# Batch 1's attention moved from the head into chunk 0's first layer

## Chip, cores, metric

The kernel runs on one core of a Trainium2 chip. The metric is device time in microseconds of one launch; lower is better. A core has TensorE (PE), VectorE (DVE), ScalarE (ACT), GpSimd (POOL) and SyncE (SP), which here only issues DMAs, and 16 DMA engines that all queues share.

## What is computed

Eight batches, eight heads, 576 positions, head size 64, float32. Linear attention without a softmax, a root-mean-square norm per head, then a gated feed-forward layer whose weights arrive as float64:

```python
kv = np.einsum('bhsd,bhse->bhde', k, v)
out = np.einsum('bhsd,bhde->bhse', q, kv)
rms = np.sqrt(np.mean(out * out, axis=-1, keepdims=True) + 1e-06)
x = (out / rms * g_norm)            # then (B,H,S,D) -> (B*S, H*D): 4608 tokens of 512
gate = 1.0 / (1.0 + np.exp(-(x @ w_gate)))      # w_gate, w_val: 512 x 1536
result = (gate * (x @ w_val)) @ w_out           # w_out: 1536 x 512
```

## The kernel before

**Chunks.** The 4608 tokens are nine chunks of 512. Chunk 0 needs batch 0, chunk 1 the end of batch 0 and most of batch 1, and so on. `xT_ring` holds three chunks of normed attention, features on the partitions. A chunk has a first layer (gate and value, 12 blocks of 128 hidden features) and a second layer. Chunk 0 is computed plainly: a block is 8 matmuls of 128x128 by 128x512 (`Plain.mm`, L561), the second layer 48 more (L808). Chunks 1 to 8 use a scheme with fewer, smaller products (L932 and L1036) of sums: sums of weights (`w1_sums` at L741, `w_form` at L1007), sums of x (`x_sums` at L830) and sums of hidden values (`h_sums` at L722). Most of these sums are GpSimd's.

**Two forms of attention.** In the *early form* (`attention`, L276 to L342) a pair of heads goes through k-v matmuls (KV), a copy (KVO), TensorE transposes of q (Q), a copy (QO), the product with q (U), Square (SQ), a sum (SUM), Sqrt (ROOT), the norm by VectorE (NORM), TensorE transposes (X) and copies into xT (XO). Batches 0 and 1 (`NE = 2 * NHP`, eight pairs) are done so in the head. In the *late form* (`feed`) a batch's k-v matmuls come at once (L366, L372), ScalarE copies them (`kv_copies`, 12 copies), VectorE transposes q in 32x32 blocks (`turn`, L383), and two pairs at a time go through `two_pairs`: `u_mm` (L407), `u_square`, two `u_sum`, `u_root`, two `u_norm` by VectorE (L425), two `x_turn` (VectorE transposes, then DMAs into xT). Batches 2 to 7 are done so beside the fast first layers of chunks 1 to 6. The result of L366 and of `u_mm` lies in one region of PSUM, `at`, with one buffer.

**Conversion of weights.** A unit is 1 MB of float64: 12 units hold the gate and value weights of one block f of chunk 0 each, then 6 hold two blocks of w_out each. SP loads a unit into one of three `st` buffers; five VectorE steps (L179, L190, L200, L204, L211 or L213) and two of ScalarE (L184, L195) make float32 of it. The last step of a unit lets SP issue the load three units on. Chunk 0's block f needs unit f converted.

**Order.** The engines run their instructions in the order in which the program writes them. The head is written out by hand as a string of tokens: `KV0` is a step of pair 0, `c1.3` and `a1.0` are conversion steps of unit 1, `w2` loads unit 2, `b0.1.2` is a matmul of block 0, `CG`, `CV`, `S` and `M` put the gate and value of blocks 0 and 1 aside and finish them later, `warm10` stands for ten matmuls of the identity with itself, which keep TensorE busy. Blocks 0 to 3 of chunk 0 are in it. Then come blocks 4 to 11 by `plain`, with a conversion step after six of the eight matmuls of each; the gate (ACT) and the product (DVE) of a block follow in the next block (`late`). After block 8 stand batch 2's k-v matmuls, after block 10 the call `w1_sums(0)`, after block 11 `w1_sums(1)`; these write their sums over `h_more`, where batch 2's k and v had been loaded. `w1_sums(2)` follows in the second layer, when all conversions have been written.

**Buffers.** Early k, v, q tiles are in the pool `first`; when its last reader is issued, `h_main` (hidden values, three tiles) and `h_more` take its place.

Of the kernel before, what the change touches and what calls it, by code (L numbers as in the profile page):

```python
# [20 lines left out]
def kernel(  # L21
# [57 lines left out]
    first = first_ctx.__enter__()  # L79


    NE = 2 * NHP
    pairs = {n: {} for n in range(B * NHP)}

    def load_kv(n):
        if n >= NE:
            return
        b, h0 = n // NHP, 2 * (n % NHP)
        for name, src in (("k", k), ("v", v)):
            t = first.tile([NP, 2, NJ * HD], FP32, tag=name, name=name)  # L90
            nc.sync.dma_start(out=t, in_=src[b, h0:h0 + 2].rearrange("h (p j) d -> p h (j d)", j=NJ))
            pairs[n][name] = t

    def load_q(n):
        if n >= B * NHP:
            return
        b, h0 = n // NHP, 2 * (n % NHP)
        if n < NE:
            t = first.tile([NP, NJ, 2, HD], FP32, tag="q", name="q")
            for e in range(2):  # L100
                nc.sync.dma_start(out=t[:, :, e, :], in_=q[b, h0 + e].rearrange("(p j) d -> p j d", j=NJ))
        else:
            t = sb.tile([NP, 2, NJ * HD], FP32, tag="q", name="q", bufs=1)
# [5 lines left out]
    def load_late(b):  # L109


        if b >= B:
            return
        mains = {}
        for n in range(NHP):
            for name, src in (("k", k), ("v", v)):
                mains[n, name] = t = kv_place(len(mains))
                nc.sync.dma_start(out=t.rearrange("p (h c) -> p h c", h=2),
                                  in_=src[b, 2 * n:2 * n + 2, 0:S4].rearrange("h (p j) d -> p h (j d)", j=NK4))
        rest = kv_place(len(mains))  # L120
        for i, src in enumerate((k, v)):
            for r in range(2):
                nc.scalar.dma_start(out=rest[PH * r:PH * r + PH, GH * i:GH * i + GH].rearrange("p (h d) -> p h d", d=HD),
                                  in_=src[b, NHP * r:NHP * r + NHP, S4:S].rearrange("h p d -> p h d"))
        kv_late[b] = mains, rest

# [91 lines left out]

    conversion = [convert(u) for u in range(len(units))]

    to_convert = deque((u, i) for u in range(5, len(units)) for i in range(5))

    def convert_step():

# [40 lines left out]
    def attention(n, at_ps):  # L265
# [12 lines left out]

        def kv_out():
            nc.vector.tensor_copy(out=kv, in_=d["kv"][:, 0, 0:HD])  # L280
            load_kv(n + 4)

        def q_mm():
            d["q"] = ps = at_ps("q")
# [5 lines left out]
        def q_out():  # L290
            d["qT"] = qTs[:, n % 2, 0:S]
            nc.scalar.copy(out=d["qT"].rearrange("p (i n) -> p i n", i=2), in_=d["q"][:, :, 0:JH * NP])
            for i in (n + 4,) if n + 4 < NE else (NE,) if n == NE - 1 else ():
                load_q(i)

        def u_mm():

# [56 lines left out]
    def feed(b):  # L354
# [25 lines left out]
        def turn(n, e):  # L380

            w_ = NJ * HD
            nc.vector.transpose(qTs[0:NP, n % 2, w_ * e:w_ * e + w_],  # L383
                                pairs[n]["q"][:, e].rearrange("p (j i c) -> p i j c", i=NC, c=QB))
            if e == 1:
                load_q(n + 1)

        def two_pairs(n0):

# [38 lines left out]
            def x_turn(i):  # L428
# [6 lines left out]
                for j in range(2):  # L435
# [7 lines left out]
                                                          in_=xTs[p0:p0 + QB, i, :, s0:s0 + n_])  # L443
                            s0 += n_

            return ([u_mm, u_square, lambda: u_sum(0), lambda: u_sum(1), u_root, lambda: u_norm(0), lambda: u_norm(1)] +
                    [lambda i=i: x_turn(i) for i in range(NC)])

        def turns_of(n):
# [3 lines left out]
        kv = [kv_mm] + [lambda i=i: kv_copies(i, range(3)) for i in range(2 * NC)]  # L453
        t0, t1, t2, t3 = (turns_of(n0 + i) for i in range(4))
        u0, u1 = two_pairs(n0), two_pairs(n0 + 2)
        steps_ = t0 + t1 + t2 + t3 + u0 + u1[:7]
        first = [(p, steps_[i]) for p, i in (((0, 0), (5, 1), (9, 2), (21, 3), (25, 8), (26, 9), (28, 4), (28, 5), (30, 10), (30, 11), (32, 6), (42, 12), (48, 13), (49, 7), (50, 14), (52, 15), (53, 16), (53, 17), (56, 18), (57, 19), (57, 20), (60, 21), (60, 22), (62, 23)) if b == 2 else
                                             ((5, 0), (8, 1), (22, 2), (24, 3), (28, 8), (29, 4), (29, 5), (30, 9), (33, 10), (33, 11), (35, 6), (36, 12), (41, 13), (47, 7), (47, 14), (51, 15), (51, 16), (54, 17), (56, 18), (56, 19), (56, 20), (61, 21), (64, 22), (64, 23)) if b == 3 else
# [64 lines left out]
    def mm_ps():  # L523
        return bank((2, 3, 0, 1)[next(turns) % 4])
# [45 lines left out]

    late = deque()

    def plain(c, u, ps):
# [17 lines left out]

    order = """
        warm10 KV0 Q0 KVO0 QO0 w1 warm3 U0 SQ0 KV1 SUM0 ROOT0 Q1 KVO1 NORM0 QO1 warm3 U1 SQ1 SUM1 X0 c0.0 c0.1
        XO0 ROOT1 NORM1 warm13 KV2 warm2 Q2 KVO2 a0.0 c0.2 X1 a0.1 c0.3 c0.4 QO2 w2 warm6 U2 SQ2 KV3 Q3 b0.0.0 b0.1.0
        KVO3 XO1 QO3 w3 U3 SUM2 KV4 Q4 ROOT2 NORM2 SQ3 SUM3 ROOT3 X2 XO2 b0.0.1 b0.1.1 b0.0.2 NORM3 X3 KVO4 QO4
        U4 c1.0 a1.0 c1.1 a1.1 c1.2 c1.3 b0.1.2 KV5 Q5 KVO5 XO3 b0.0.3 b0.1.3 SQ4 c1.4 w4 SUM4 QO5 U5 CG0 CV0
        KV6 Q6 b1.0.0 ROOT4 NORM4 X4 b1.1.0 b1.0.1 b1.1.1 SQ5 SUM5 ROOT5 KVO6 QO6 XO4 U6 NORM5 X5 c2.0 c2.1 a2.0
        c2.2 b1.0.2 KV7 Q7 SQ6 SUM6 a2.1 b1.1.2 ROOT6 c2.3 b1.0.3 XO5 b1.1.3 KVO7 QO7 U7 c2.4 NORM6 CG1 X6 CV1  # L600
        b2.0.0 SQ7 XO6 b2.1.0 b2.0.1 c3.0 SUM7 ROOT7 b2.1.1 c3.1 a3.0 a3.1 NORM7 X7 XO7 c3.2 c3.3 c3.4 b2.0.2
        b2.1.2 b2.0.3 c4.0 S0 S1 b2.1.3 M0 G2 M1 b3.0.0 b3.1.0 a4.0 E2 c4.1 a4.1 c4.2 c4.3 b3.0.1 b3.1.1 b3.0.2
        b3.1.2 b3.0.3 b3.1.3 c4.4
    """
    blks, copies = {}, {}
    warm = mm0_ps()
    for token in order.split():
        name = token.rstrip("0123456789.")
        n = [int(i) for i in token[len(name):].split(".")]
        f = n[0]  # L610
        if name == "b":
            if f not in blks:
                if f == 3:
                    psum_ctx.__exit__(None, None, None)
                    psum = ctx.enter_context(tc.tile_pool(name="psum", bufs=1, space=bass.MemoryType.PSUM))
                    ps = (mm_ps(), mm_ps())
                else:
                    ps = (mm0_ps() if f else warm, mm0_ps())
                blks[f] = Plain(0, F_ORDER[f], ps)
            blks[f].mm(n[1], n[2])  # L620
        elif name == "CG":
            copies[f, 0] = sg_tile()
            nc.scalar.copy(out=copies[f, 0], in_=blks[f].ps[0])
        elif name == "CV":
            copies[f, 1] = sg_tile()
            nc.vector.tensor_copy(out=copies[f, 1], in_=blks[f].ps[1])
        elif name == "S":
            nc.scalar.activation(out=copies[f, 0], in_=copies[f, 0], func=AF.Sigmoid)
        elif name == "M":
            nc.vector.tensor_tensor(out=gv_tile(0, F_ORDER[f]), in0=copies[f, 1], in1=copies[f, 0], op=ALU.mult)  # L630
        elif name == "G":
            blks[f].gate()
        elif name == "E":
            blks[f].end()
        elif name in ("c", "a"):
            conversion[f][name][n[1]]()
        elif name == "w":
# [145 lines left out]
    w1_more[0] = [more[:, i] for i in range(10)]  # L783
    w1_more[1] = [more[:, i] for i in range(10, 18)] + [sgs[-1][:, GH * i:GH * i + GH] for i in range(2)]
    spare_sg = sgs.pop()
    second_batch = feed(2)
    load_late(2)
    late.extend([blks[3].gate, blks[3].end])
    for f in range(4, NFT):
        if f == NFT - 1:  # L790
            last = at_ps()
            plain(0, f, (last[:, 0], last[:, 1]))
        else:
            plain(0, f, (mm_ps(), mm_ps()))
        if f == 8:
            second_batch[0][0]()
        elif f == 9:
            for step in second_batch[0][1:]:
                step()
        elif f == 10:  # L800
            w1_sums(0)
        elif f == NFT - 1:
            w1_sums(1)

    ps = [mm_ps() for _ in range(G // P)]
# [359 lines left out]
```

## Time and profile before

| | us |
|---|---|
| median of three runs | 1016.38 (1016.28 to 1017.71) |
| the profiled execution's own time | 1015.84 |
| its span | 1014.1 |
| TensorE busy | 1006.5 (99%) |
| VectorE busy | 727.1 (72%) |
| GpSimd busy | 598.9 (59%) |
| ScalarE busy | 350.2 (35%) |
| last early attention step on TensorE (L333) | 52.7 |
| batch 2's k-v matmuls (L366, L372) | 98.0 to 100.4 |
| chunk 0's second layer on TensorE (L808) | 121.1 to 162.3 |
| chunk 1 | 162.3 to 269.9 |

The span runs from the first to the last instruction of one profiled execution. A timeline row reads: start, duration, engine, line, operation, output<-input, shape; in brackets the idle time of the engine before it and what ended that. One matmul of the program is two in the trace[...]. An entry "PE" is the multiplication, "PEld" the loading of weights beside it. The pitch of one instruction to the next can be less than its duration where two overlap, so sums are made from starts.

### The profile page before, as it was taken

The numbers are of one execution on the slowest core, as the hardware profiler recorded it, in microseconds if no ns is written. First come the engines' busy times: TensorE is split into PE (matmuls) and PEld (weight loads), VectorE is DVE, ScalarE is ACT, GpSimd is POOL, SyncE is SP. The second block draws the span as 40 slices with busy tenths as digits, with TensorE's granted clock in tenths as the row PEclk, the third lists the DMA queues.
The fourth block names the chain that finished last, engine by engine and source line by source line (L and its number), as shares of the span: only waits on it lengthen the run. The fifth ranks groups of instructions, "written<-read, shape, count | busy, mean of one in ns | idle before, by whom it ended". The sixth has DMA issues, their size and how long they took to land.

```text
span 1014.1 us, 18347 instructions
## 1 busy us (share of the span) xinstructions
PE 1006.5 (99%) x6914; PEld 828.0 (82%) x6914; DVE 727.1 (72%) x1211; ACT 350.2 (35%) x609; POOL 598.9 (59%) x965
## 2 busy tenths in 40 slices
PE   9999999999999999999999999999999999999998
PEld 8644447888888888888888888888888888888887
DVE  4899899899668846775678666866688556755672
ACT  4654422442154304441254115421453033213320
POOL 0001999998448642967177706962496439744963
PEclk9999999999999999999999999999999999999999
DMA  9975314644778468646765577556764546444514
GB/s 264 278 237 191 125 42 157 220 143 163 235 245 301 165 194 262 225 159 200 232 234 194 150 229 248 195 160 190 235 214 153 178 155 208 161 156 158 211 59 124
DMA packets 101128, 193.89 MB, mean 191 GB/s; under 512 B 27408, under 2 KB 74128, under 8 KB 101040
## 3 DMA queue, kind: packets, MB, share of 16 engines
q0 software_dynamic: 20976, 112.87, 32.9%
q1 hardware_dynamic: 72896, 77.75, 25.2%
q10 hardware_dynamic: 7168, 2.10, 0.9%
q8 instruction: 55, 0.90, 0.4%
q14 instruction: 33, 0.27, 0.1%
HBM read 160.04 MB, written 25.56 MB: 183 GB/s over the span
## 4 chain that ended last, share of the span: by engine, by line
PE 74%; POOL 2%; issue 0%; DVE 0%; POOLq 0%
PE mm L932 47%; PE mm L1036 24%; PE at L407 2%; PE at L366 1%; POOL h L722 1%; POOL w_ring L1007 0%; POOL h_more L722 0%; PE at L372 0%; POOL w L770 0%; DVE sg L902 0%; POOL w L1007 0%; POOLq L1007 0%
## 5 line engine op out<-in xcount | busy, mean ns | idle before, releaser
L932 PE MATMUL mm<-xs,w 128*128 128x256 f32 x1428 | 332.0, 380 | 0.0
L932 PEld LDWEIGHTS mm<-xs,w 128*128 128x128 f32 x1428 | 270.4, 190 | 37.4 <-DVE temps L902 0.3
L932 PE MATMUL mm<-xT,w 128*128 128x256 f32 x948 | 230.0, 380 | 0.0
L932 PEld LDWEIGHTS mm<-xT,w 128*128 128x128 f32 x948 | 179.4, 190 | 25.5 <-issue 1.0
L902 DVE TENSOR_TENSOR sg<-sg,mm 128x512 f32<-128x512 f32 (+1 forms) x176 | 100.8, 599 | 93.1 <-PE mm L932 45.7
L770 POOL DMA_DIRECT2D w<-kept x84 | 46.9, 558 | 190.7 <-PE mm L932 188.4
L1036 PE MATMUL mm<-w,h 128*128 128x256 f32 x630 | 143.4, 379 | 0.9 <-POOL h L894 0.5
L1036 PEld LDWEIGHTS mm<-w,h 128*128 128x128 f32 x630 | 119.5, 190 | 17.9 <-POOL h L894 0.9
L898 ACT COPY temps<-mm 128x512 f32<-128x512 f32 (+1 forms) x128 | 66.0, 537 | 190.0 <-PE mm L932 94.9
L894 POOL TENSOR_TENSOR h<-h,sg 128x512 f32<-128x512 f32 x72 | 97.6, 1372 | 50.3 <-DVE h L902 33.2
L722 POOL TENSOR_TENSOR h<-h 128x128 f32<-128x128 f32 x216 | 113.4, 537 | 16.5 <-DVE h_more L722 13.1
L1036 PE MATMUL mm<-w,h_more 128*128 128x256 f32 x474 | 108.2, 379 | 0.0
L891 ACT ACTIVATE sg<-sg 128x512 f32<-128x512 f32 x96 | 59.7, 630 | 131.4 <-DVE sg L902 131.4
L1036 PEld LDWEIGHTS mm<-w,h_more 128*128 128x128 f32 x474 | 90.1, 190 | 12.2
L898 ACT COPY sg<-mm 128x512 f32<-128x512 f32 (+1 forms) x112 | 57.1, 510 | 91.2 <-PE mm L1036 48.8
L722 POOL TENSOR_TENSOR h_more<-h 128x128 f32<-128x128 f32 x120 | 58.5, 490 | 33.9 <-DVE h L894 29.6
L561 PE MATMUL mm<-xT,w 128*128 128x512 f32 x176 | 77.7, 594 | 0.0
L902 DVE TENSOR_TENSOR temps<-temps,mm 128x512 f32<-128x512 f32 (+1 forms) x96 | 59.2, 617 | 25.5 <-PE mm L1036 17.2
L902 DVE TENSOR_TENSOR temps<-mm,temps 128x512 f32<-128x512 f32 (+1 forms) x64 | 39.8, 621 | 50.6 <-PE mm L1036 23.6
L898 ACT COPY h<-mm 128x512 f32<-128x512 f32 x48 | 28.1, 585 | 125.5 <-PE mm L932 110.5
L902 DVE TENSOR_TENSOR sg<-mm,sg 128x512 f32<-128x512 f32 (+1 forms) x64 | 39.6, 618 | 43.7 <-PE mm L932 21.9
L741 POOL TENSOR_TENSOR h_more<-w 128x256 f32<-128x256 f32 x10 | 12.8, 1299 | 97.4 <-PE at L366 97.4
(132 smaller groups left out, 1324.5 us busy)
## 6 DMA issues: line engine op xcount, KB each, us to landing
w<-kept POOLq DMA_DIRECT2D x42, 896.0 KB, 5.0
w<-kept POOLq DMA_DIRECT2D x90, 384.0 KB, 4.6
w<-kept POOLq DMA_DIRECT2D x42, 768.0 KB, 5.4
q<-in_q_dram SPq DMA_DIRECT2D x24, 288.0 KB, 3.0
out_dram<-sg SPq DMA_DIRECT2D x104, 64.0 KB, 1.7
st<-in_moe_w_gate_dram SPq DMA_DIRECT2D x12, 512.0 KB, 5.5
st<-in_moe_w_val_dram SPq DMA_DIRECT2D x12, 512.0 KB, 6.6
h_more<-in_k_dram SPq DMA_DIRECT2D x24, 256.0 KB, 5.0
```

Of the source, the lines that this page charges most:

```text
L366: nc.tensor.matmul(ps[HD * e:HD * e + HD, n // 2, n % 2], mains[n, "k"][:, c], mains[n, "v"][:, c], start=(n % 2 == 0 and j == 0), stop=Fa ...
L407: nc.tensor.matmul(u[HD * e:HD * e + HD, r, o:o + HD], qTs[QB * r:QB * r + QB, (n0 + which) % 2, c:c + PH], kvq[QB * r:QB * r + QB, (n0 + ...
L561: nc.tensor.matmul(self.ps[i], w[("wg", "wv")[i], self.f][:, m, :], xT[self.c][:, m, :], start=(m == 0), stop=(m == NMT - 1), skip_group_c ...
L722: ops.append((eng, lambda v=v, x=x, sign=sign, y=y, eng=eng: eng.tensor_tensor(out=h_form(v, j), in0=h_form(x, j), in1=h_form(y, j), op=op ...
L741: nc.gpsimd.tensor_tensor(out=w1_slot(j, w_at[v]), in0=w1_slot(j, w_at[x]), in1=w1_slot(j, w_at[y]), op=op_of(sign))
L770: nc.gpsimd.dma_start(out=granule(g)[:, 0:n], in_=kept1[g // NPA % N3, g % NPA][:, 0:n])
L891: nc.scalar.activation(out=o["o" + step[1]], in_=o["o" + step[1]], func=AF.Sigmoid)
L894: mult.tensor_tensor(out=o[x], in0=o[x], in1=o[y], op=ALU.mult)
L898: nc.scalar.copy(out=o[out_], in_=o[expr])
L902: tt(out=o[out_], in0=o[x], in1=o[y], op=ALU.add if sign == "+" else ALU.subtract)
L932: nc.tensor.matmul(regions[name][1][:, g], ws[:, g], xf[c][wv], start=(new and g == 0), stop=True, skip_group_check=True)
L1036: nc.tensor.matmul(regions[name][1], h_form(hv, j), ws[:, j], start=(used[i] and j == 0), stop=(j == N3 - 1), skip_group_check=True)
```

## The change

Batch 1 leaves the head: `NE` is 4 pairs. It is done in the late form, in chunk 0's first layer. Its q tiles lie in parts of `h_main` that are not written yet, its k and v in `h_more` ahead of batch 2's. Its norm is 18 small activations of ScalarE with a pointer scale per two pairs in place of VectorE's `u_norm`. The head's order is new and has block 0 alone; blocks 1 to 11 go through `plain`. All that stands beside their 88 matmuls is one list by place: place p is the p-th matmul from block 1 on, after which the named steps are written (`CV` a conversion step; `LL`, `LL2` loads of k and v of batch 1 and 2; `Q0` a load of q; `t00` a turn; `KV`, `C0` the k-v matmuls and copies of batch 1; `au` to `ax1` and `bu` to `bx1` the steps of the two `two_pairs`, `n0` to `n2` being the norm; `KV2`, `D0` those of batch 2; `W0` is `w1_sums(0)`). Batch 1's outputs are stored in the later batches' pieces of 32 rows.

```diff
-    NE = 2 * NHP
+    NE = NHP
...
+            if b == 1:
+                i = n - NE
+                t = h_main[2 - i // 2].rearrange("p s c -> p (s c)")[0:NP, (i % 2) * 2 * NJ * HD:(i % 2 + 1) * 2 * NJ * HD]
+                t = t.rearrange("p (h c) -> p h c", h=2)
+            else:
+                t = sb.tile([NP, 2, NJ * HD], FP32, tag="q", name="q", bufs=1)
...
-                nc.scalar.dma_start(out=rest[PH * r:PH * r + PH, GH * i:GH * i + GH].rearrange("p (h d) -> p h d", d=HD),
+                (nc.sync if b == 1 else nc.scalar).dma_start(out=rest[PH * r:PH * r + PH, GH * i:GH * i + GH].rearrange("p (h d) -> p h d", d=HD),
...
-    to_convert = deque((u, i) for u in range(5, len(units)) for i in range(5))
+    to_convert = deque((u, i) for u in range(2, len(units)) for i in range(5))
...
-            return ([u_mm, u_square, lambda: u_sum(0), lambda: u_sum(1), u_root, lambda: u_norm(0), lambda: u_norm(1)] +
+            def norm(r):
+                for n in range(NJ):
+                    nc.scalar.activation(out=by_head(sq)[:, r, n], in_=by_head(d["u"])[:, r, n], func=AF.Copy,
+                                         scale=ms[:, r, n:n + 1])
+
+            if b == 1:
+                norms = [lambda: nc.vector.reciprocal(ms, ms)] + [lambda r=r: norm(r) for r in range(NQ)]
+            else:
+                norms = [lambda: u_norm(0), lambda: u_norm(1)]
+            return ([u_mm, u_square, lambda: u_sum(0), lambda: u_sum(1), u_root] + norms +
                     [lambda i=i: x_turn(i) for i in range(NC)])
...
+        if b == 1:
+            return kv, t0 + t1 + t2 + t3 + u0 + u1, ()
...
-            if b < 2:
+            if b < NE // NHP:
...
-            if at < 6:
-                convert_step()
+            for step in steps_at.get(at, ()):
+                step()
...
+    order = """w1 warm9 KV0 Q0 KVO0 QO0 U0 warm8 SQ0 SUM0 ROOT0 KV1 Q1 KVO1 NORM0 warm5 X0 QO1 U1 SQ1 XO0 c0.0 SUM1 ROOT1 c0.1 warm14 NORM1 KV2 warm2 Q2 a0.0 c0.2 KVO2 a0.1 c0.3 c0.4 QO2 X1 warm2 U2 SQ2 KV3 Q3 b0.0.0 KVO3 SUM2 w2 w3 XO1 QO3 U3 ROOT2 NORM2 c1.1 SQ3 a1.1 X2 b0.0.1 SUM3 c1.0 ROOT3 XO2 b0.1.0 b0.1.1 NORM3 X3 b0.1.2 a1.0 c1.3 c1.2 b0.0.2 c1.4 w4 XO3 b0.0.3 b0.1.3
+    """
...
-    second_batch = feed(2)
-    load_late(2)
-    late.extend([blks[3].gate, blks[3].end])
-    for f in range(4, NFT):
+    batch1, second_batch = feed(1), feed(2)
...
+    places = """
+        1:CV,CV 2:CV,Q1 4:CV,CV 5:CV,CV 6:CV,LL,Q0 7:CV,CV 10:CV,CV 11:Q2 13:Q3 15:CV 16:CV,CV 17:t10
+        18:CV,CV 19:t00,t01 20:KV 21:t11 22:CV,CV,C1 23:CV,C0,C2,C3 25:CV 26:CV,CV 29:au,t20,t21,LL2 30:CV
+        31:t30,asq 32:CV,as0 33:t31 34:CV,as1,art 35:CV 36:arc,an0 37:an1 38:CV,an2 40:CV,CV 41:CV,ax0 43:ax1
+        44:bu 46:CV,bsq 48:CV,CV,bs0 50:CV 52:CV,CV 54:bs1 55:CV,CV,brt 57:CV,CV 58:CV 60:CV,brc 62:bn0,bn1
+        63:bn2 64:CV 65:CV,CV,CV 66:CV,CV 67:CV 68:KV2,D2 69:D3 70:D0,D1 71:bx0 72:CV 73:W0 75:bx1
+        80:CV,CV,CV,CV,CV 84:CV 87:CV,CV
+    """
...
+    for f in range(1, NFT):
         if f == NFT - 1:
             last = at_ps()
...
+        plain(0, f, ps, {at: at_place.get(2 * NMT * (f - 1) + at, ()) for at in range(2 * NMT)})
+        if f == NFT - 1:
             w1_sums(1)
```

More of the change, by code (lines that the diff above doesn't have):

```diff
@@ L102, in load_q @@
         else:
-            t = sb.tile([NP, 2, NJ * HD], FP32, tag="q", name="q", bufs=1)
+            if b == 1:
[4 more added lines that the diff above has]
+                t = sb.tile([NP, 2, NJ * HD], FP32, tag="q", name="q", bufs=1)
             nc.sync.dma_start(out=t, in_=q[b, h0:h0 + 2].rearrange("h (p j) d -> p h (j d)", j=NJ))
@@ L280, in kv_out @@
             nc.vector.tensor_copy(out=kv, in_=d["kv"][:, 0, 0:HD])
-            load_kv(n + 4)
         def q_mm():
@@ L292, in q_out @@
             nc.scalar.copy(out=d["qT"].rearrange("p (i n) -> p i n", i=2), in_=d["q"][:, :, 0:JH * NP])
-            for i in (n + 4,) if n + 4 < NE else (NE,) if n == NE - 1 else ():
-                load_q(i)
         def u_mm():
@@ L385, in turn @@
             if e == 1:
-                load_q(n + 1)
+                if b > 1:
+                    load_q(n + 1)
+                elif n == 2 * NHP - 1:
+                    load_q(n + 1)
         def two_pairs(n0):
@@ L571, with plain @@
     late = deque()
-    def plain(c, u, ps):
+    def plain(c, u, ps, steps_at):
         f = F_ORDER[u]
@@ L590 @@
              "NORM": U_NORM, "X": X, "XO": X_OUT}
[L594 to L603, printed above, removed]
+    order = """w1 warm9 KV0 Q0 KVO0 QO0 U0 warm8 SQ0 SUM0 ROOT0 KV1 Q1 KVO1 NORM0 warm5 X0 QO1 U1 SQ1 XO0 c0.0 SUM1 ROOT1 c0.1 warm14 NORM1 KV2 warm2 Q2 a0.0 c0.2 KVO2 a0.1 c0.3 c0.4 QO2 X1 warm2 U2 SQ2 KV3 Q3 b0.0.0 KVO3 SUM2 w2 w3 XO1 QO3 U3 ROOT2 NORM2 c1.1 SQ3 a1.1 X2 b0.0.1 SUM3 c1.0 ROOT3 XO2 b0.1.0 b0.1.1 NORM3 X3 b0.1.2 a1.0 c1.3 c1.2 b0.0.2 c1.4 w4 XO3 b0.0.3 b0.1.3
     """
-    blks, copies = {}, {}
+    blk = None
     warm = mm0_ps()
@@ L611 @@
         if name == "b":
[L612 to L634, printed above, removed]
+            blk = blk or Plain(0, F_ORDER[0], (warm, mm0_ps()))
+            blk.mm(n[1], n[2])
         elif name in ("c", "a"):
@@ L785 @@
     spare_sg = sgs.pop()
-    second_batch = feed(2)
-    load_late(2)
-    late.extend([blks[3].gate, blks[3].end])
-    for f in range(4, NFT):
+    batch1, second_batch = feed(1), feed(2)
+    named = {"LL": lambda: load_late(1), "LL2": lambda: load_late(2), "KV": batch1[0][0], "KV2": second_batch[0][0],
+             "W0": lambda: w1_sums(0), "CV": convert_step}
+    for i in range(NHP):
+        named.update({f"Q{i}": lambda i=i: load_q(NE + i), f"C{i}": batch1[0][1 + i], f"D{i}": second_batch[0][1 + i]})
+        named.update({f"t{i}{e}": batch1[1][2 * i + e] for e in range(2)})
+    for i, which in enumerate("ab"):
+        for n, step in enumerate(("u", "sq", "s0", "s1", "rt", "rc", "n0", "n1", "n2", "x0", "x1")):
+            named[which + step] = batch1[1][2 * NHP + 11 * i + n]
+    places = """
[6 more added lines that the diff above has]
+    """
+    at_place = {}
+    for some in places.split():
+        p, names = some.split(":")
+        at_place[int(p)] = [named[name] for name in names.split(",")]
+    psum_ctx.__exit__(None, None, None)
+    psum = ctx.enter_context(tc.tile_pool(name="psum", bufs=1, space=bass.MemoryType.PSUM))
+    late.extend([blk.gate, blk.end])
+    for f in range(1, NFT):
         if f == NFT - 1:
             last = at_ps()
-            plain(0, f, (last[:, 0], last[:, 1]))
+            ps = last[:, 0], last[:, 1]
         else:
[L794 to L802, printed above, removed]
+            ps = mm_ps(), mm_ps()
+        plain(0, f, ps, {at: at_place.get(2 * NMT * (f - 1) + at, ()) for at in range(2 * NMT)})
+        if f == NFT - 1:
             w1_sums(1)
```

## Prediction

> **What bounds the kernel now.** I read the page first (engine shares, chain of waits), then the stage table, the chain in order of time, and the timelines of TensorE, GpSimd, VectorE and ScalarE from 0 to 330 us. TensorE is busy almost without a gap, and the chain ends on it. But the chain's last entry before the long TensorE run is GpSimd:
>
> ```profile
> PE   9999999999999999999999999999999999999998
> POOL 0001999998448642967177706962496439744963
> ...
> 259.83 0.46 POOL h L722
> 260.29 0.04 issue
> 260.34 9.76 PE mm L1036 x44
> ```
>
> From 260.34 us on, only TensorE is on the chain: whatever moves that point moves the end. Before it the chain runs on GpSimd back to 240 us. The GpSimd timeline shows why:
>
> ```profile
> 98.74 0.73 POOL L741 TENSOR_TENSOR h_more<-w 128x256 f32<-128x256 f32 x1 [97.43 <-PE at L366]
> ...
> 182.07 0.72 POOL L741 TENSOR_TENSOR sg<-sg,w_ring 128x256 f32<-128x256 f32 x1
> 182.76 1.27 POOL L894 TENSOR_TENSOR h<-h,sg 128x512 f32<-128x512 f32 x1
> 185.70 6.22 POOL L894 TENSOR_TENSOR h<-h,sg 128x512 f32<-128x512 f32 x3 [1.67 <-DVE h L902]
> ```
>
> GpSimd starts its weight sums (L741) at 98.74, released by batch 2's k-v matmuls (L366, start 97.98), because the sums are written over those k and v. It does 76 sums, then chunk 1's products and h sums. Up to 235 us it waits once, 1.67 us. TensorE hangs on it in that stretch: at 217.52 ScalarE's copy into an sg tile waited 1.42 us for GpSimd to finish reading it, and TensorE at 218.16 waited 0.74 us for that copy. So two clocks run: TensorE's own work, and "start of the sums plus GpSimd's queue". The second is the later one. How fast the queue runs depends on VectorE:
>
> ```profile
> 98.74:152.76 54.02, 54.02 (x184) 24.79 (x181) 49.58 (x39) 21.20 (x29) 53.16 (x41) 1.00 0.27 92
> 152.76:182.76 30.00, 30.00 (x118) 22.22 (x117) 27.59 (x38) 8.50 (x15) 29.29 (x37) 1.00 0.47 151
> ```
>
> Columns: stretch, its length, busy time of TensorE, weight loads, VectorE, ScalarE, GpSimd. The timeline counts 40 sums in the first stretch (1.35 us each), while VectorE converts weights, and 36 in the second (0.83 us each). VectorE's last conversion step ends at 152.2.
>
> [...] 1.35 against 0.83 us on GpSimd, and VectorE's L179 takes 0.69 us before the sums and 1.21 during them. [...] here the load is 1.28 and the next activation starts 0.01 us later, so I use 1.28. [...]
>
> **TensorE's work.** By starts in the timeline, an early pair costs 0.85 (L276) + 0.55 (L287) + 0.74 (L306) + 0.55 (L333) = 2.69 us; four go: -10.8. The late form adds one set of k-v matmuls (97.98 to 100.38, 2.4 us) and two L407 sets (184.83 to 186.61, 1.75 each): +5.9. Warm-up matmuls go from 37 to 40 at 0.23: +0.7. Net -4.2 us.
>
> **The new head, added up in queue order.** The start is as before to Q0 (7.7). KVO0, QO0: U0 at 8.77, as now. Eight warm-ups, KV1, Q1 to 12.75; KVO1 now stands ahead of NORM0 on VectorE, so NORM0 ends 14.3, X0 at 14.5 (now 12.86), U1 to 15.8. Fourteen warm-ups to 19.0, KV2, Q2, X1 to 21.4. KVO2 and QO2 behind Q2: U2 at 22.0; KV3, Q3, first matmul to 25.0; U3 to 26.05; NORM2 ends 26.8, X2 at 27.0; from there TensorE is full (X2, 3 matmuls, X3, 4 matmuls at 0.865): block 1 starts at **34.2**. That is 30.1 us of start and work and 4.1 of waits; the same bookkeeping for the present kernel leaves 2.3 of waits up to 121.09. So the gain of the head is 4.2 - 1.8: the second layer could start at 34.2 + 11 blocks x 6.92 + 5.9 + 2.4 = 118.6, **2.5 us earlier**. My sums are good to some 1.5 us.
>
> **The attention inside the first layer.** A place is one matmul, 0.865 us. Weights: VectorE needs 4.8 us per unit by starts (0.60, 0.61, 1.14, 1.25, 1.20) plus 0.6 for the gate product, against 6.92 us of TensorE per block; unit 2 is done at 39.6 (block 2 starts 41.1), unit 3 at 45.0 (48.0), later units with 4 to 8 us to spare, also with eight turns (0.5), four sums (0.7) and the x transposes. I cost these at nothing; without that cover they would be 10 us. Loads: SP issues batch 1's k and v (12 DMAs, 0.4 to 0.6 each) behind unit 5's load, about 40.5 to 50; 3.3 MB at some 270 GB/s (early slices) land near 53 to 54, and the k-v matmuls at place 20 start at 52.4 and use them over 2.4 us: 0.3, between 0 and 2. Q0, units 6 and 7, Q2 and Q3 queue behind them and come in time, Q0 perhaps 1 us late for VectorE only. ScalarE issues four batch 2 DMAs (0.63 each), which wait for unit 7's load: hidden by VectorE still busy.
>
> The norm by ScalarE is an operation that the trace lacks. 18 activations of 64 elements with a pointer scale: [...] bounds 2.2 (the 128x64 copy in L342 overlapped at 0.12) [...]. It saves VectorE 1.5 us per two pairs (two L425 at 0.75) and adds Sqrt and Sigmoid table loads, 2.56 us. First round: sums end 71.3, table and root 73.3, reciprocal, a conversion step, norm 74.4 to 78.8. The gate of block 5 waits behind it (to 80.7, in time for block 7), and so does *bu* at place 44: it needs the one attention region of PSUM, which the norm still reads, and TensorE is there at 77.3. **TensorE waits 1.5 us** (0 to 3.5). Second round: norm ends near 101, and KV2 at place 68 wants the same region.
>
> **When GpSimd starts.** KV2 starts at 34.2 + 69 x 0.865 + 2.4 + 3.5 + 0.3 + 1.5 = 101.6 (now 97.98): the head is shorter, but KV2 stands half a block later and 5.9 us of attention is ahead of it. The sums start 0.76 after, at **102.3, 3.6 later**. VectorE also has six gate products and transposes to place between conversions; reckoned in queue order, with the durations of this stretch (unit 7.3 us), its last unit ends at 154.9 instead of 152.2. Each wo unit is then ready 0 to 2 us before TensorE needs it. GpSimd: 102.3 to 154.9 is 52.6/1.35 = 39.0 sums, the other 37.0 x 0.83 take 30.9: done at 185.8 instead of 182.8, **+3.0**. The 1.67 us wait takes its part: **+1.3 us** at 185.7 and, with queue and coupling unchanged, at 260.34 and at the end. TensorE's 0.7 us that is left of the head (2.5 - 1.8) waits with it.
>
> Edits at nothing: finer stores of chunks 1 and 2 (7 and 1 more SP DMAs of 0.45): the next k and v land about 284 for a use at 289; the cover is 5 us. Batch 1's xT arrives by DMA near 112 for x sums near 155. The conversion list's own order: VectorE's slack above.
>
> **Sum.** The profiled execution took 1015.84 (span 1014.1), 0.54 below the median of three. The change against it is +1.3, so 1017.7 against the median of 1016.38 (1016.38 + 1.3). A measurement can tell about 0.2% (2.0 us) from no change, so this is "no change", on its slow side. Its own range is 1015.2 to 1018.4.
>
> **Rivals.** *Slower*: the PSUM region decides. If 18 activations cost over 5 us or a gate or root stands badly, *bu* and KV2 are each held longer; a further 2.5 us gives sums at 104.8 and conversions to 157: +5.3 - 1.7 = +3.7, 1020.1. It turns from "same" at 0.8 us of further delay, which speaks for it; against it, ScalarE is busy 35%. *Faster*: my waits are too high. A head 2 us shorter and no wait at *bu* put the sums at 98.5 and conversions at 149.7: the sums end 1.4 us earlier, the 1.67 us are taken from that too (-3.1, TensorE's own 4.5 us leave room), 1013.3. For it: KV2 and conversions both lie on queues that I added up pessimistically, semaphore by semaphore. *Late k and v*: if they land 3 us late the head's gain is gone; each us of later start costs 0.83/1.35 us with the conversions not held up: +1.9 more, 1019.6. That the norm isn't moved is out: the listing of the instruction order shows 36 activations on ScalarE.
>
> **How the numbers follow.** No change 0.40, slower 0.40 (the region 0.28, late data 0.12), faster 0.20. The range reaches from the faster case to beyond the slower one: 1013.3 to 1021.5.
>
> **What would show it.** Right: block 1 near 34, a TensorE wait at *bu* near 77, the sums starting 2 to 5 us later than 98.74, no wait for VectorE at the second L894, chain again over GpSimd before 260. Wrong: sums at or before 98.74, or GpSimd idle in 185 to 235.

## The result: 0.45% slower, by a stop of TensorE that the forecast had no term for

| | before | after |
|---|---|---|
| median, runs side by side | 1016.33 us (1016.17 to 1017.71) | 1021.03 us (1019.60 to 1022.36) |
| ratio, 95% interval | | 1.0045 (1.0031 to 1.0058) |
| the profiled execution, its span | 1015.84, 1014.1 | 1022.36, 1020.6 |

The change costs 4.7 us; 1.3 had been forecast. The profiled execution of after is the slowest of its four runs, so its span is longer by 6.5 us, more than the medians.

The page of after, busy tenths of TensorE and GpSimd, and the end of its chain of waits (start, duration, engine, what):

```profile
PE   8998999999999999999999999999999999999998
POOL 0000799998628661867078615963396539743963
```
```profile
265.50 0.46 POOL h L708
265.96 0.04 issue
266.00 9.76 PE mm L1037 x44
275.77 13.45 PE mm L933 x63
289.22 7.52 DMA h_more<-in_v_dram
```

The point from which TensorE carries the chain is still handed over by GpSimd, at 266.00 in place of 260.34, 5.66 us later; 0.6 us more is a wait for the next batch's k and v (the DMA in the last line, taken up below). GpSimd's timeline shows the start of the weight sums (now L727) and of chunk 1's products (now L895):

```profile
107.94 0.73 POOL L727 TENSOR_TENSOR h_more<-w 128x256 f32<-128x256 f32 x1 [106.62 <-PE at L368]
...
190.00 7.53 POOL L895 TENSOR_TENSOR h<-h,sg 128x512 f32<-128x512 f32 x4
```

The sums start 9.2 us later, not 3.6, and are done at 190.00, 7.24 later. The four products run through: the 1.67 us wait for VectorE is gone, as forecast. 7.24 - 1.67 = 5.57, against 5.66 at the handover. So the way from the sums to the end is the forecast one; the delay arose before 107. TensorE's timeline from 59 us on (L412 is `u_mm`, L577 the plain matmuls, L368 the k-v matmuls):

```profile
59.59 3.17 PE L577 MATMUL mm<-xT,w 128*128 128x512 f32 x7
62.69 1.92 PE L412 MATMUL at<-kvq,qTs 32*64 32x64 f32 x144
64.54 13.14 PE L577 MATMUL mm<-xT,w 128*128 128x512 f32 x30
77.61 1.78 PE L412 MATMUL at<-kvq,qTs 32*64 32x64 f32 x140
83.60 0.48 PE L412 MATMUL at<-kvq,qTs 32*64 32x64 f32 x4 [4.20 <-issue]
84.01 23.23 PE L577 MATMUL mm<-xT,w 128*128 128x512 f32 x48
107.17 2.08 PE L368 MATMUL at<-h_more 128*64 128x64 f32 x64
```

TensorE reaches `bu` about when it was reckoned to (77.3 forecast, 77.61 measured) and begins it at once. It does 140 of the 144 entries of `bu` and stands still for 4.2 us before the last four, which is called the gap from here on; "issue" means that nothing the profile shows released it. The next 48 matmuls take 23.16 us (84.01 to 107.17) where 48 usual pitches are 20.8. The stage table tells why (columns: stretch, its length, busy time of TensorE, weight loads, VectorE, ScalarE, GpSimd, granted clock, DMA share, GB/s):

```profile
76.00:80.00 4.00, 3.40 (x144) 2.03 (x143) 2.57 (x6) 3.97 (x10) 0.00 (x0) 1.00 1.11 254
80.00:84.00 4.00, 0.40 (x4) 0.28 (x3) 3.75 (x6) 1.53 (x2) 0.00 (x0) 0.75 0.85 236
84.00:88.00 4.00, 4.00 (x6) 1.85 (x6) 0.75 (x1) 1.62 (x2) 0.00 (x0) 0.50 0.75 238
```

The granted clock is 0.5 from 82.0 to 88.8 us, which costs 2.4 us on top of the 4.2 in this execution. The DMA engines are saturated when the gap begins (79.4 us): their share is 1.11 from 76 to 80 us.

### The profile page after: what moved, and what is told of

Read it like the earlier page. It is cut to its first block, busy times and chain, and to the rows that moved or that the text cites. A ratio compares the mean times of both kernels' runs of the same rounds, so it can differ in the third digit from the quotient of the medians.

```text
span 1020.6 us, 18562 instructions
## 1 busy us (share of the span) xinstructions
PE 1006.4 (99%) x6988; PEld 826.0 (81%) x6988; DVE 727.4 (71%) x1215; ACT 360.6 (35%) x639; POOL 597.9 (59%) x965
## 4 chain that ended last, share of the span: by engine, by line
PE 73%; POOL 2%; DMA 1%; issue 0%; DVE 0%; POOLq 0%
PE mm L933 46%; PE mm L1037 24%; PE at L412 2%; POOL h L708 1%; PE at L368 1%; DMA h_more<-in_v_dram 1%; POOL w_ring L1008 0%; POOL h_more L708 0%; PE at L374 0%; POOL w L756 0%; DVE sg L903 0%; POOL w L1008 0%; POOLq L1008 0%
## 5 line engine op out<-in xcount | busy, mean ns | idle before, releaser
L895 POOL TENSOR_TENSOR h<-h,sg 128x512 f32<-128x512 f32 x72 | 97.7, 1376 | 49.5 <-DVE h L903 32.2
L577 PE MATMUL mm<-xT,w 128*128 128x512 f32 x176 | 79.5, 610 | 0.0
L727 POOL TENSOR_TENSOR h_more<-w 128x256 f32<-128x256 f32 x10 | 11.9, 1208 | 106.6 <-PE at L368 106.6
```

Of the source, the lines that this page charges most:

```text
L577: nc.tensor.matmul(self.ps[i], w[("wg", "wv")[i], self.f][:, m, :], xT[self.c][:, m, :], start=(m == 0), stop=(m == NMT - 1), skip_group_c ...
L727: nc.gpsimd.tensor_tensor(out=w1_slot(j, w_at[v]), in0=w1_slot(j, w_at[x]), in1=w1_slot(j, w_at[y]), op=op_of(sign))
L895: mult.tensor_tensor(out=o[x], in0=o[x], in1=o[y], op=ALU.mult)
```

## What stood behind the gap: the theories

**Instruction supply.** The traces of before and after each have a DMA queue of kind "instruction" with 55 transfers of 16 KB. TensorE has 14,077 records in before and 14,231 in after, its sequencer's included: 256 and 259 to a transfer. From the start of one transfer to the start of the next it gets through 252 records in before and 254 in after, in the mean. So my estimate is a block of some 256 of TensorE's instructions to a transfer, and the theory is that TensorE stands still when it has used up one block before the next has come; no record shows a block being used up. A program matmul is four records here (two multiplications and two weight loads); a plain one takes 0.865 us, so by the estimate a block lasts some 55 us. `bu` is 72 program matmuls, 288 records in 1.8 us: more than a block. In after one of the 16 KB transfers starts at 80.89, inside the gap.

**Rivals.** The PSUM region: `bu`, the norm by ScalarE and the k-v matmuls hold one another up (the slower rival of the prediction). Speed alone, a variant of the first theory: the block would be late without other transfers too.

## Experiments

All ratios are to the kernel before, run side by side.

**1. `bu` five places later**

```diff
-        44:bu 46:CV,bsq 48:CV,CV,bs0 50:CV 52:CV,CV 54:bs1 55:CV,CV,brt 57:CV,CV 58:CV 60:CV,brc 62:bn0,bn1
+        46:CV 48:CV,CV 49:bu 50:CV,bsq 52:CV,CV,bs0 54:bs1 55:CV,CV,brt 57:CV,CV 58:CV 60:CV,brc 62:bn0,bn1
```

> The changed kernel with bu (the second pair of pairs' attention matmuls) at place 49 in place of 44, its squares and first sum at 50 and 52. Instruction supply (the 4.2 us of idle TensorE inside bu is a block of 256 instructions that arrives late, because bu uses up 288 instructions in 1.8 us just after the block before it was used up): five more plain matmuls, 20 instructions and 4.3 us, stand ahead of bu, so the block is there: no idle time over 1 us inside bu, granted clock 1.00 from 76 to 92 us, batch 2's k-v matmuls start near 101 (now 107.2), the weight sums near 102, and the whole is 4 to 6 us shorter than the changed kernel's 1021.0: 1015 to 1017. PSUM region (bu, the norm by ScalarE and the k-v matmuls hold one another up through their common region): bu later brings nothing, the idle time stays inside or ahead of bu or moves to the k-v matmuls, the sums start at 106 or later: 1020 to 1023.

Measured: 1016.06 us, 0.9997 (0.9988 to 1.0006). Its TensorE timeline, stage table and GpSimd timeline:

```profile
63.78 17.43 PE L577 MATMUL mm<-xT,w 128*128 128x512 f32 x40
81.14 2.04 PE L412 MATMUL at<-kvq,qTs 32*64 32x64 f32 x144
83.11 16.57 PE L577 MATMUL mm<-xT,w 128*128 128x512 f32 x38
99.61 2.09 PE L368 MATMUL at<-h_more 128*64 128x64 f32 x64
```
```profile
80.00:84.00 4.00, 4.00 (x149) 2.49 (x148) 3.92 (x6) 2.33 (x3) 0.00 (x0) 1.00 0.44 111
84.00:88.00 4.00, 4.00 (x11) 1.77 (x10) 4.00 (x6) 2.91 (x4) 0.00 (x0) 1.00 0.88 276
```
```profile
100.38 1.08 POOL L727 TENSOR_TENSOR h_more<-w 128x256 f32<-128x256 f32 x1 [99.07 <-PE at L368]
...
183.53 7.52 POOL L895 TENSOR_TENSOR h<-h,sg 128x512 f32<-128x512 f32 x4
```

No gap, the full clock (1.00), all 144 matmuls in one row (the plain row ahead of it has 40 entries in place of 30, the five program matmuls of the edit); the sums start 7.6 us earlier than in after. The same work with one burst five places later (its squares and first sum move with it) is 5 us shorter and level with before.

**2. Batch 2's k and v asked for behind `bu`**

```diff
-        18:CV,CV 19:t00,t01 20:KV 21:t11 22:CV,CV,C1 23:CV,C0,C2,C3 25:CV 26:CV,CV 29:au,t20,t21,LL2 30:CV
+        18:CV,CV 19:t00,t01 20:KV 21:t11 22:CV,CV,C1 23:CV,C0,C2,C3 25:CV 26:CV,CV 29:au,t20,t21 30:CV
...
-        44:bu 46:CV,bsq 48:CV,CV,bs0 50:CV 52:CV,CV 54:bs1 55:CV,CV,brt 57:CV,CV 58:CV 60:CV,brc 62:bn0,bn1
+        44:bu 46:CV,bsq,LL2 48:CV,CV,bs0 50:CV 52:CV,CV 54:bs1 55:CV,CV,brt 57:CV,CV 58:CV 60:CV,brc 62:bn0,bn1
```

> The changed kernel with batch 2's k and v (LL2, 12 transfers of 2.3 MB) asked for at place 46 in place of 29, behind bu; bu stays at 44. Instruction supply, late through the transfers in front of it: between 70 and 81 us there is less to carry, the block arrives at once, the idle time in bu is under 1.5 us, clock 1.00, sums start 101 to 104, 1015 to 1018. Instruction supply, late through bu's speed alone: the idle time stays at 3 us or more, 1020 to 1022. PSUM region: no change, 1020 to 1022.

Measured: 1020.31 us, 1.0039 (1.0026 to 1.0052); 2.92 us of idle time before the last four matmuls of `bu`. A miss for the transfers as I had them. The DMA engines were idle from 73 to 76.9 us, but SP had issued a 1 MB weight load at 76.2 and 76.6, and the block's transfer began at 80.68, as that burst ended. Either it was speed alone, or the load that mattered was this one.

**3. The norm by VectorE**

```diff
-                norms = [lambda: nc.vector.reciprocal(ms, ms)] + [lambda r=r: norm(r) for r in range(NQ)]
+                norms = [lambda: u_norm(0), lambda: u_norm(1), lambda: None, lambda: None]
```

> The changed kernel with the second batch's norm by VectorE (two multiplications of 0.75 us each in place of 18 activations of ScalarE), all else as it is. Instruction supply: TensorE's order and the transfers are the same, so the idle time in bu stays at 3 to 5 us, the sums start at 106 to 109, 1019 to 1023. PSUM region: the region is free 2 to 3 us earlier in both rounds, the idle time at bu goes or halves, sums start by 105, 1016 to 1019.

Measured: 1016.64 us, 1.0006 (0.9997 to 1.0016); idle time 0.60 us. This is what the PSUM rival had said, not what I had. But TensorE began `bu` no earlier (77.84 against 77.61). What had moved was the weight load: VectorE, busy with the norm, freed its buffer later, SP issued it at 77.0 and 77.4 in place of 75.2 and 75.6, and the block's transfer started at 77.75, ahead of it. The next two separate these readings.

**4. Three conversion steps behind `ax0`**, which delays that load and leaves the norm on ScalarE:

```diff
-        31:t30,asq 32:CV,as0 33:t31 34:CV,as1,art 35:CV 36:arc,an0 37:an1 38:CV,an2 40:CV,CV 41:CV,ax0 43:ax1
+        31:t30,asq 32:CV,as0 33:t31 34:CV,as1,art 35:CV 36:arc,an0 37:an1 38:CV,an2 41:ax0 42:CV,CV,CV 43:ax1
```

> The changed kernel with the three conversion steps of places 40 and 41 put behind ax0 at place 42: the last of them frees the buffer for the 1 MB weight load that SP issued at 75.2 and 75.6 us, so that load is issued some 2 us later. bu, the norm on ScalarE and TensorE's order stay. Instruction supply behind the load (in the four kernels seen the block's transfer begins only when a burst of loads ends, and the one kernel whose load was issued at 77.0 had it at 77.8): the block slips in ahead of the load, idle time in bu under 1.2 us, clock 1.00, sums start 100 to 103.5, 1015 to 1018. PSUM region: the norm and bu are as before, idle time 3 to 5 us, 1019.5 to 1022.5.

Measured: 1019.27 us, 1.0025 (1.0017 to 1.0034). The load was issued at 82.0. TensorE, and the DMA queues (packets, MB, share of the 16 engines; packets count by their start, so that a share can pass 100%) from 78.5 to 80 us of this kernel, then from 77 to 80.8 and from 80.8 to 82.2 us of after:

```profile
77.66 1.81 PE L412 MATMUL at<-kvq,qTs 32*64 32x64 f32 x140
81.18 0.33 PE L412 MATMUL at<-kvq,qTs 32*64 32x64 f32 x4 [1.70 <-issue]
81.44 22.56 PE L577 MATMUL mm<-xT,w 128*128 128x512 f32 x48
```
```profile
q1 hardware_dynamic: 77, 0.07, 19.7%
q8 instruction: 1, 0.02, 5.2%
```
```profile
q1 hardware_dynamic: 1006, 1.04, 111.4%
```
```profile
q1 hardware_dynamic: 338, 0.32, 89.0%
q8 instruction: 1, 0.02, 5.2%
```

With the DMA engines at 47% from 76.5 to 78.6 us and nearly free after that, the block's transfer starts 0.9 us after `bu` does (78.57 against 77.66), not 3.3 as in after, and the gap is 1.7, not 4.2. So I was half right: with that load out of the way the gap is 2.5 us shorter, but it does not go. That the remaining 1.7 us is the speed of the burst alone is not shown: in experiment 3, with the DMA engines at 93% from 76 to 77.7 us, the block started 0.09 us before `bu` and the gap was 0.60. The norm is untouched and the gap shrank: the PSUM region is not its cause.

**5. Five warm-up matmuls fewer in the head**

```diff
-    order = """w1 warm9 KV0 Q0 KVO0 QO0 U0 warm8 SQ0 ...
+    order = """w1 warm9 KV0 Q0 KVO0 QO0 U0 warm3 SQ0 ...
```

> The changed kernel with three warm-up matmuls in place of eight ahead of the first norm: every later instruction of TensorE has a number that is 20 smaller, bu stays at place 44, the norm stays on ScalarE, the transfers stay. Instruction supply: the idle time sat 278 instructions into bu's 288; it stays at the same number of instructions and so moves out of bu, 10 instructions behind it, into or behind the third plain matmul after bu. Those matmuls take 2 of the 4.2 us: idle time of 1 to 3 us there and none inside bu, and some 2 us less on the whole: 1017.5 to 1020. PSUM region or another wait that belongs to bu: the idle time stays inside bu at 3 to 5 us, 1020 to 1022.

Measured: 1017.90 us, 1.0013 (1.0002 to 1.0024). The gap left `bu`: all 144 matmuls ran through from 76.81. Of the 1 to 3 us behind it nothing over 0.3 was seen (the block's transfer began at 78.85). But the 20 instructions moved every later boundary too, and another burst of L412, in chunk 4, now met one:

```profile
512.53 1.75 PE L412 MATMUL at<-kvq,qTs 32*64 32x64 f32 x136
515.86 0.34 PE L412 MATMUL at<-kvq,qTs 32*64 32x64 f32 x8 [1.59 <-issue]
```

A 16 KB transfer starts at 513.3, 0.8 us after that burst. Against experiment 1, which has no such gap, the kernel is 1.8 us longer (2.3 by the profiled spans: 0.5 of it is there at the last handover, 1.6 is this gap). Warm-up matmuls at 9 us decide over a gap at 514.

**6. `bu` in halves**, two plain matmuls between them:

```diff
-            def u_mm():
-                d["u"] = u = at_ps()[:, 0:NQ, 0:2 * QC]
-                for which in range(2):
+            def u_mm(parts=(0, 1)):
+                if 0 in parts:
+                    d["u"] = at_ps()[:, 0:NQ, 0:2 * QC]
+                u = d["u"]
+                for which in parts:
...
-        44:bu 46:CV,bsq 48:CV,CV,bs0 ...
+        44:bu 46:bv,CV,bsq 48:CV,CV,bs0 ...
```

> The changed kernel with bu cut in two: its first 36 matmuls (144 instructions) at place 44, the other 36 at place 46, two plain matmuls (8 instructions, 1.7 us) between them. Number of instructions, norm and transfers stay. Instruction supply: the idle time stays about 278 to 286 instructions behind the start of bu, so it now lies in the last eighth of the second half, and as the burst has 1.7 us more time while the block is under way it is 1.7 us shorter: 2 to 3 us in place of 4.2, if the block comes as late as before; the whole 2 to 4 us less, 1017 to 1019.5. PSUM region or another wait that belongs to the start of bu: the first half is hit like the whole was, 3.5 to 5 us idle inside or right behind the first half, 1020 to 1022.

Measured: 1017.02 us, 1.0011 (1.0000 to 1.0022). Here `u_mm` is L414, the plain matmuls L583:

```profile
77.06 1.05 PE L414 MATMUL at<-kvq,qTs 32*64 32x64 f32 x72
78.04 1.98 PE L583 MATMUL mm<-xT,w 128*128 128x512 f32 x4
79.95 0.95 PE L414 MATMUL at<-kvq,qTs 32*64 32x64 f32 x64
81.93 0.34 PE L414 MATMUL at<-kvq,qTs 32*64 32x64 f32 x8 [1.03 <-issue]
```

The gap comes behind 72 + 64 = 136 matmul records of `bu` (in after behind 140; the two plain matmuls between the halves are the other 4), so at the same count, in the second half and not at the start of `bu`, and is 1.0 us; the block came 1 us earlier than in after, and the 1.9 us between the halves covered most of the rest. The clock stayed at 1.00 in this execution (1016.60 us). But 6 of the 20 executions took 1019.8 to 1021.7 us at a mean clock of 0.994 to 0.997; what they met was not profiled, so the halves are no sure cure.

**7. The changed kernel once more**

> The changed kernel once more, unedited, for a second profile. Instruction supply: the idle time lies at the same instruction of bu (278 of 288); its length goes with the start of the block's transfer (2.5 us from that start to TensorE's next instruction) and may differ from 4.2 us by a microsecond: 1019 to 1022. A chance event of the one profiled execution: no idle time in bu, 1016 to 1018.

Measured: 1020.73 us, 1.0042 (1.0028 to 1.0055). The gap stands before the same four matmuls, 2.74 us long, and the clock is halved for 3.4 us. So it is no chance event, and its length varies.

The gap in one table (us; the load is the second half of the 1 MB load nearest to `bu`; "offset" is the start of the block's transfer from the start of `bu`; the last column is the median less experiment 1's 1016.06):

| kernel | load issued | block starts | `bu` starts | offset | idle | lost |
|---|---|---|---|---|---|---|
| after | 75.64 | 80.89 | 77.61 | 3.28 | 4.20 | 5.0 |
| 7, the same again | 77.75 | 81.75 | 79.71 | 2.04 | 2.74 | 4.7 |
| 2, k and v later | 76.62 | 80.68 | 78.53 | 2.15 | 2.92 | 4.2 |
| 4, load later | 82.54 | 78.57 | 77.66 | 0.91 | 1.70 | 3.2 |
| 3, norm by VectorE | 77.41 | 77.75 | 77.84 | -0.09 | 0.60 | 0.6 |
| 1, `bu` later | 74.91 | 80.17 | 81.14 | -0.97 | 0 | 0 |

In the five with a gap, idle time is offset + 0.7 to 0.9: TensorE goes on 2.5 to 2.7 us after the transfer's start, and the burst had work for 1.8. Where a load had been issued a microsecond or more ahead of `bu`, the block started 4.0 to 5.3 us after that load. The time lost is about the idle time plus the halved clock: 1.7 + 1.7 for the fourth row, 2.7 + 1.7 for the second (22.5 us for the 48 matmuls in both, in place of 20.8). In the first row it is less than 4.2 + 2.4, since the idle time is that of the slowest execution and the loss that of the median.

The count of instructions settles what the gap belongs to. When all records of TensorE in a trace are numbered in order of their start (its sequencer's included), 1729 come before the gap in after and in experiments 2, 3, 4, 6 and 7, and 7873 before the one at 515.86 in experiment 5. They lie 6144 records apart, which is 24 times 256 (1729 is 6 x 256 + 193, 7873 is 30 x 256 + 193): the same place in a block of 256, in two chunks, at different matmuls of a burst. In experiment 5 that place had moved out of `bu`, 13 records behind its end.

**8. Batch 2's k-v matmuls four places later, without the gap** (against experiment 1)

```diff
-        63:bn2 64:CV 65:CV,CV,CV 66:CV,CV 67:CV 68:KV2,D2 69:D3 70:D0,D1 71:bx0 72:CV 73:W0 75:bx1
+        63:bn2 64:CV 65:CV,CV,CV 66:CV,CV 67:CV 72:CV,KV2,D2 73:D3 74:D0,D1 75:bx0 77:W0 79:bx1
```

> The kernel with bu at 49, and with batch 2's k-v matmuls at place 72 in place of 68 (copies, first weight sums and transposes with them). Two clocks: sums start 3.5 us later (103.9), done 2.1 us later (185.7), last long TensorE run from 261.6: 1018.2. TensorE alone sets the end: 1015.5 to 1016.5.

Measured: 1017.71 us, 1.0012 (1.0003 to 1.0021). Sums start 103.71 (+3.33), done 184.60 (+1.07), last handover 260.88 (+1.43), time +1.65. The direction is the two clocks'; the price is 0.32 us per us of later start at the end of the sums, half of the 0.62 that I had used, and 0.43 at the handover.

**9. The same matmuls four places earlier** (against experiment 1)

```diff
-        46:CV 48:CV,CV 49:bu 50:CV,bsq 52:CV,CV,bs0 54:bs1 55:CV,CV,brt 57:CV,CV 58:CV 60:CV,brc 62:bn0,bn1
-        63:bn2 64:CV 65:CV,CV,CV 66:CV,CV 67:CV 68:KV2,D2 69:D3 70:D0,D1 71:bx0 72:CV 73:W0 75:bx1
+        46:CV 48:CV,CV 49:bu 50:CV,bsq 52:CV,CV,bs0 53:bs1 54:brt 55:CV,CV 56:brc 57:CV,CV,bn0 58:CV,bn1 59:bn2 60:CV
+        64:CV,KV2,D2 65:CV,CV,CV,D3 66:CV,CV,D0,D1 67:CV,bx0 69:W0 71:bx1 72:CV
```

> The kernel with bu at 49, and with the second round's sums, root and norm up to four places earlier and batch 2's k-v matmuls at place 64 in place of 68 (copies, first weight sums and transposes with them). Two clocks: the sums start 3.5 us earlier (96.9 against 100.38); with VectorE's conversions as they are, each us is worth 0.83/1.35 = 0.62, so the sums are done at 181.4 in place of 183.5 and the last long TensorE run ahead of the end starts at 257.3 in place of 259.45: 1013.9. TensorE alone sets the end: no change from 1016.1. VectorE becomes the bound (it converts beside GpSimd for longer and each step is slower): a wait of GpSimd for VectorE comes back at chunk 1's products, gain under 1 us, 1015 to 1016.5.

Measured: 1015.91 us, 0.9995 (0.9988 to 1.0002): no gain over experiment 1. TensorE and GpSimd:

```profile
97.81 2.09 PE L368 MATMUL at<-h_more 128*64 128x64 f32 x64 [1.42 <-ACT sqs L453]
```
```profile
98.57 1.10 POOL L727 TENSOR_TENSOR h_more<-w 128x256 f32<-128x256 f32 x1 [97.26 <-PE at L368]
...
183.00 1.28 POOL L895 TENSOR_TENSOR h<-h,sg 128x512 f32<-128x512 f32 x1
184.97 6.23 POOL L895 TENSOR_TENSOR h<-h,sg 128x512 f32<-128x512 f32 x3 [0.69 <-DVE h L903]
```

Two waits take the gain. The PSUM region does bind here: the k-v matmuls waited 1.42 us for ScalarE's norm (L453). And the wait for VectorE ahead of the second product is back.

**10. Chunk 1's first four products by VectorE, on experiment 1's kernel and on before**

```diff
-                combine(o, regions, steps, nc.vector if j == N3 - 1 and i == NPR - 1 else nc.gpsimd)
+                combine(o, regions, steps, nc.vector if (c, j) == (1, 0) or (j == N3 - 1 and i == NPR - 1) else nc.gpsimd)
```

> The kernel with bu at 49, and with the four 128x512 products of chunk 1's first third on VectorE (0.7 us each) in place of GpSimd (7.5 us together at 183.5). Two clocks: GpSimd's queue is 7.5 us shorter from 183.5 on, so TensorE's waits that hang on it between 190 and 260 (gaps of 1.0, 1.1, 0.8 and 0.8 us where 0.2 is usual, 2.9 us in all) go, and nothing takes their place: 1013 to 1014. VectorE becomes the bound (its products wait for ScalarE's sigmoid and hold up what is queued behind them): TensorE waits for VectorE's combinations instead, gain under 1 us or a loss, 1015.3 to 1017.5. TensorE alone sets the end: no change from 1016.1.

Measured: **1014.80 us, 0.9990 (0.9982 to 0.9999)**, the shortest median of the study; the margin over before is only just outside its error. By the medians it is 1.3 us under experiment 1, by the ratios 0.7, and the two intervals overlap.

> The kernel before with the same edit: the four products of chunk 1's first third on VectorE in place of GpSimd. Two clocks: TensorE's gaps at 217.0, 235.5 and 259.5 (1.1, 0.85 and 0.8 us where 0.2 is usual, 2.1 us in all) go: 1014 to 1014.7, still longer than the same edit with the attention moved, because TensorE's own clock is the earlier one there. TensorE alone or VectorE as the bound: 1015.5 to 1017.5.

Measured: 1016.14 us, 0.9996 (0.9987 to 1.0004), no gain. The waits of TensorE (us in total, times, longest) from 150 to 264 us show the difference. The first two lines are of before without and with the edit, the second two of experiment 1 without and with it:

```profile
PE mm L932 <- ACT sg L898: 0.7, 1, 0.7
PE mm L932 <- DVE sg L902: 0.9, 1, 0.9
```
```profile
PE mm L933 <- ACT sg L899: 1.4, 2, 0.8
PE mm L933 <- DVE sg L903: 0.7, 1, 0.7
```

With the products gone from GpSimd, TensorE's waits for ScalarE's copies go and one for VectorE comes. Before had 0.7 us of them to lose and got 0.9 back; experiment 1's kernel had 1.4. All waits of that stretch together go from 1.6 to 1.7 us in before and from 2.5 to 1.4 in experiment 1's kernel. With the attention moved TensorE starts chunk 1 2.7 us earlier (159.63 against 162.29), which may be why it has more of these waits; that was not tested.

**11. Before, with batch 2's k-v matmuls a block later**

```diff
-        if f == 8:
+        if f == 9:
             second_batch[0][0]()
-        elif f == 9:
+        elif f == 10:
             for step in second_batch[0][1:]:
                 step()
-        elif f == 10:
-            w1_sums(0)
         elif f == NFT - 1:
+            w1_sums(0)
             w1_sums(1)
```

> The kernel before with batch 2's k-v matmuls, their copies and the first weight sums one block (6.9 us) later; nothing else. Two clocks (the start of GpSimd's weight sums plus its queue sets the point from which TensorE alone is on the chain): sums start near 105.7; VectorE's conversions end at 152 as now, so the sums are done 6.9 x 0.83/1.35 = 4.3 us later, the 1.67 us wait for VectorE is taken up, and the end is 2.6 us later: 1019.0, the last long TensorE run starts near 263. TensorE alone sets the end: no change, 1015.5 to 1017.

Measured: 1020.97 us, 1.0047 (1.0032 to 1.0062). Inconclusive: the last block of the first layer uses the same PSUM region, and TensorE waited 3.1 us in it for ScalarE's copies of k-v, with a halved clock behind that. Experiments 8 and 9 took its place.

## Why the prediction held in its range and failed in its mechanism

**Luck.** The measured 1021.03 us lies inside the range of 1013.3 to 1021.5, but nothing in the prediction led there. The likeliest case was "no change", 1015.2 to 1018.4; the measured 0.45% (0.31 to 0.58) is more than the 0.2% that the prediction itself called measurable. The range reached so far for the sake of rivals that did not come. Of the signs of being right, block 1 at 34, the missing wait for VectorE and the chain over GpSimd (until 266) came; the sums started 9.2 us later, not 2 to 5, and the stop at `bu` was not the wait that was meant.

**The step that failed** is the wait at `bu`. I priced it at 1.5 us (0 to 3.5) from the one semaphore that I knew there, the norm. That wait was under 0.1: the norm began at 73.65, not 74.4, took 3.79 us, not the 4.4 of my estimate (74.4 to 78.8), and ended as TensorE arrived. What stood there was of another kind, a late block of instructions: 2.7 to 4.2 us in the two profiles of this kernel, and 1.7 to 2.4 through the clock. My account of queues had no line for TensorE's own instruction stream. Without the gap (experiment 1) the result is "no change", as the likeliest case had it, but 1.6 us below its 1017.7: neither the wait of 1.5 us at `bu` nor the 0.3 for batch 1's k and v is in the trace of after.

**Right.** Block 1 at 34.2: 34.3 in after. Batch 1's k-v matmuls at 52.4: 52.36. Chunk 0's second layer "could start at 118.6": 118.43 in experiment 1 (125.99 in after). The table load of 1.28 us with the next activation right behind:

```profile
71.10 1.28 ACT L424 ACT_TABLE_LOAD   x1
72.39 0.31 ACT L424 ACTIVATE ms<-ms,eps 128x18 f32<-128x18 f32 x1
73.65 3.79 ACT L453 ACTIVATE sqs<-at,ms 128x64 f32<-128x64 f32 x18
```

The two clocks and the 1.67 us: in after 7.24 - 1.67 against 5.66 at the handover, in experiment 1 0.77 - 1.67 = -0.90 against -0.89.

**Mis-sized.** The sums were to start at 102.3; without the gap 100.38. VectorE was to end its conversions at 154.9; in experiment 1 it did at 151.4, earlier than before's 152.2. The price of a late start was 0.32 in experiment 8, while the gap, which holds up TensorE, VectorE and GpSimd together, costs its full length (in experiment 7, 2.74 us and 1.7 by the clock, for 4.7 lost). *Slower*, my rival, gave nearly the right time (1020.1) for the wrong reason: the region held `bu` up by less than 0.1 us.

**The finer stores.** I gave them a cover of 5 us. In after SP issued the next k and v from 284.0 (before: from 273.0), and TensorE waited 0.6 us for them at 296.9, which is the 0.6 us beyond the handover; in experiment 1 they were issued from 275.5 and nobody waited. So there was no cover left once the sums were late. How much of this the stores themselves add was not tried.

**Open.** When the transfer of a block is asked for, and why it comes so late behind a load, the trace does not show; experiment 5's small cover, some 0.5 us better than the table's rule gives, is not explained either.

## What to carry to other kernels

Here a burst of 72 small matmuls (288 instructions in 1.8 us, against some 256 to a block) stood idle for up to 4.2 us, and no semaphore showed why: look for "issue" in front of a matmul inside a burst, and for the 16 KB transfers of the instruction queue beside it. The gap hung on the count of all instructions before it (20 fewer at 9 us took it out of `bu`, and one of 1.59 us came at 514) and on the loads under way (4.20 us with a load just ahead of `bu`, 1.70 with that load later), so an edit far off can bring or remove one; cut the burst, move it, or keep large loads from being issued just ahead of it (each of these shortened the gap here, to 1.03, 0 and 1.70 us; only the move took it away). Judge a change of order only after such a gap has been taken out: this one was worth nothing and looked like a loss of 5 us.

## What the runs showed of the hardware

- TensorE went on 2.5 to 2.7 us after the start of a block's 16 KB transfer (itself 1.2 us): 2.61 in experiment 4, with the DMA engines nearly free (the queues at 19.7% and 5.2% from 78.5 to 80 us), and 2.71 in after (at 89.0% and 5.2% from 80.8 to 82.2 us).
- The gaps of 0.6 to 4.2 us in bursts came at one place of a count in 256 instructions (193), in seven traces (after and experiments 2 to 7).
- The clock was halved for 3.4 us (6.8 in after) behind idle times of TensorE of 1.7, 2.7, 2.9 and 4.2 us (experiments 4, 7, 2 and after; mean clock of the execution 0.998, 0.997, 0.996 and 0.997), and of 2.0 and 3.1 us in before with the edits of experiments 10 and 11 (0.998 in both). It was not halved behind 1.6 us (experiment 5; 0.999) or 1.0 us (experiment 6; 1.000). An idle time of 1.0 us in the head was followed by it in experiments 2 and 7 and not in after. Why 1.0 us was followed by it in two traces and not in another was not shown.
- Pointer-scale activations of 64 elements on ScalarE started 0.197 us apart (3.79 us for 18).
